# One conditional block ahead of the expert slots in place of four behind them

## Chip, cores, metric

One Trainium2 chip, one core. The metric is device time in microseconds of one execution.

## What is computed

Three stages in a row, all in float32 at the interface (the second MLP's weights come as float64):

```python
# 1: attention, q, k, v: [4, 8, 576, 64]
out_d = softmax_attention(mean of 4 tokens of q, of k, of v)      # 144 tokens
scores = np.where(abs(i - j) < 4, scale * q @ k.T, -1e9)
attn_out = repeat(out_d, 4) + softmax(scores) @ v
x = attn_out.transpose(0, 2, 1, 3).reshape(2304, 512)
# 2: mixture of 8 experts, one expert per row
e_idx = argmax(x @ w_gate + modality_bias[modality_id])
for e in range(8):
    h = np.maximum(x[e_idx == e] @ w1[e], 0)                        # 512 -> 1024
    out[e_idx == e] = gate_w * (h @ w2[e])                          # 1024 -> 512
# 3: MLP 512 -> 2048 -> 512
h = out @ w_in
g = np.maximum(h, 0) + alpha * np.minimum(h, 0)
return g @ w_out
```

## The kernel before

Line numbers are those of the kernel before.

**Attention** (to L371) yields after each tile of 96 tokens; it writes each row with its gate to a table in DRAM (xs), sorted by expert. Beside it class `Early` (L569 to L596) already works out slots of 128 rows of the leading expert (ph and py are its matmuls, L583).

**Plan.** At the end of the attention `Router.plan` (L444 to L498) counts the rows of each expert on DVE, and writes a table of integers (r_tab): for each slot of 256 rows its expert, its first row, where its result goes, and, in row 4, how many slots there are. Engines read single values of it into registers (`reg`, `finish`).

**Slots** (`moe`, L598 to L673). A slot is 256 rows of one expert. There are always seven (NSU = 7); up to 16 can occur (NSM), if the rows fall badly over the experts. [...] A slot: load its rows (L, L554), times the gates on POOL (L560), transpose on DVE (T, L562), split (xh, xl); eight groups h of 12 matmuls of 128x256 (L648), relu into hh and hl; four groups y of 24 (L667). 8 x 12 + 4 x 24 = 192 matmuls. Its eight pieces of w1 and eight of w2 are split one by one, a little ahead of their use; the raw weights of the next expert (wraw) are loaded into the same buffer as soon as a part is split. For slot 0 the leading expert's raw weights lie there since the attention.

**Input weights.** `W2in(i)` (L802 to L807) brings one of 32 pieces (128x256) of w_in through a ring of three buffers, makes a float32 of the float64 in three DVE operations (xwi, `from64`, L537 to L539), and splits it into wih (ACT) and wil (POOL). Each slot asks for six pieces (L654), behind its first six h groups; the scheduler puts them where operands and buffers allow.

**The end of the slots.** Behind slot 6 (L817 to L820) stand three conditional blocks for the slots past the seventh, and a fourth that loads the second MLP's first block of rows again if few early slots were done. With the data of the case none is taken. All five engines carry each block's instructions, so each branches over them.

**Second MLP** (`moe2`, L694 to L747): five blocks of rows; per block 16 groups oh (12 matmuls of 128x512, L723) and the products oy (L714). Output weights are converted during block 0.

The instruction order on each engine is set by a list scheduler at build time, within priorities (`high_priority`); conditional blocks are barriers that it doesn't move work across.

```python
            for s in range(NSU):
                if s==2: load()
                slot(s)
            for u in range(2): w_out_rows(0,u)
            # slots that are rarely there, in groups; one without rows does no harm
            for a,b in [[NSU,NSU+1],[NSU+1,NSU+3],[NSU+3,NSM]]:
                with tc.If(nb>a):
                    for s in range(a,b): slot(s)
            with tc.If(done<BLOCKS[0][1]//SE): load()
```

Of the kernel before, what the change touches and what calls it, by code (L numbers as in the profile page):

```python
# [14 lines left out]

def attention(ctx, tc, q, k, v, mod, wg, bias, xs, running, ps, eps, zeros, filler):
    """Attention, gating and the scatter of the rows by expert; yields after each token tile."""
# [87 lines left out]
    # routing constants  # L105
# [73 lines left out]
    def softd(b,name,e,p,n):  # L179
        """exp and the factors; p: n heads of scores"""  # L180
# [8 lines left out]
    def stageB(b,pair):  # L189
        """queries 0-127 of two heads"""  # L190
# [8 lines left out]
    def stageT(b):  # L199
        """the queries past 128 of all heads, on partitions (h,i)"""  # L200
# [75 lines left out]
    def local2(b,t):  # L276
        """values, the sum of both attentions"""
# [11 lines left out]
    def gate2(b,t):  # L289
        """rows and their experts"""  # L290
# [23 lines left out]
    def gate3(b,t):  # L314
        """to their places"""
# [20 lines left out]
    def down(b):  # L336
        """the work that a sequence needs before its tiles, in small steps"""
# [3 lines left out]
    # prologue  # L341
# [32 lines left out]
LEAD=1; WLOAD=tuple([0, 0, 1, 2, 2, 3, 3, 4]); EARLY=tuple([3, 6, 10, 14, 16]); ETAIL=0  # L374
F=1024; F2=2048; SL=256; SE=128; NSP=len(EARLY); NK=N//SL; NSU=-(-(N-SE*NSP)//SL); NSM=N//SL+E-1   # early slots of SE rows; slots always there, at most
ENG=mybir.EngineType

class Router:
    """Slots of 256 rows of one expert, worked out on partition 0."""
    def __init__(self, tc, rp, cp):  # L380
# [24 lines left out]
        self.done=rp.tile([1,1],I32,name="r_done"); self.tab0=rp.tile([1,4],I32,name="r_tab0")  # L405
# [4 lines left out]
    def lead(self, psum, running):  # L410
        """the expert with the most rows so far goes first"""
# [10 lines left out]
    def early(self, psum, running, k):  # L422
        """whether the leading expert has SE*(k+1) rows by now, and where they begin"""
# [7 lines left out]
        # SE*k rows into its own rows, or the zeros behind them all  # L431
# [4 lines left out]
    def early_rows(self):  # L436
        """rows of the leading expert that were worked out early"""
        nc=self.nc; dn=self.dn=self.cp.tile([1,1],F32,name="r_dn")
        nc.vector.tensor_reduce(out=dn,in_=self.ok[:,1:],axis=AX.X,op=ALU.add)
        nc.vector.tensor_copy(self.done,dn)  # L440
        nc.vector.tensor_scalar(out=dn,in0=dn,scalar1=float(SE),scalar2=None,op0=ALU.mult)
    def plan(self, psum, running, cp):
# [3 lines left out]
        nr=w([1,2,E],"nr")            # slots and rows of each expert, in the order of the slots  # L446
# [39 lines left out]
        xr=w([1,NSM],"xr")            # its rows; the zeros where there is no slot  # L486
# [10 lines left out]
        nc.vector.tensor_copy(tab[:,4,0:1],sb[:,2,E-1:E])  # L497
        nc.vector.tensor_copy(tab[:,5:7],y[:,5:7])     # where zeros go behind fewer rows than a slot's  # L498
    def reg(self, row, s, engines, hi):
        t=self.tab[0:1,row*NSM+s:row*NSM+s+1]  # L500
        if s==0 and row in (1,2,5,6): i=(1,2,5,6).index(row); t=self.tab0[0:1,i:i+1]
        return self.nc.values_load(t,engines=engines,min_val=0,max_val=hi,
            skip_runtime_bounds_check_because="follows from the row counts")
    def finish(self, engines):
        return self.nc.values_load(self.done[0:1,0:1],engines=engines,min_val=0,max_val=NSP,
            skip_runtime_bounds_check_because="a count of early slots")

class Weights:
    """One expert's weights as they come, and the parts of each chunk of 128 hidden units."""
# [4 lines left out]
    def load1(self, part, e, cond=None):  # L514
        """part 0-3: a quarter of the hidden units"""
# [4 lines left out]
    def load2(self, part, e, cond=None):  # L520
        """part 0-3: a quarter of the columns"""
# [5 lines left out]
def split(nc, hi, lo, x, lo_engine):  # L527
    """x as the sum of two parts of 12 bits each"""
# [3 lines left out]
def from64(nc, pool, name, hi, lo, raw, lo_engine):  # L532
    """float64 bits to the two parts of the float32 they give"""
# [8 lines left out]
class Rows:  # L542
    """Rows of one expert, and their result's way out."""
# [13 lines left out]
    def turn(self, pool, L, name, n):  # L557
        """times the gates, transposed"""
# [10 lines left out]
class Early:  # L569
    """Slots of the leading expert while the attention still runs, in float32 as it is."""  # L570
# [27 lines left out]
def moe(tc, stack, router, wts, rows, ep, W2in):  # L598
# [6 lines left out]
    def load_x(s):  # L605
        rows.zeros(router.reg(5,s,[ENG.SP],E*N),router.reg(6,s,[ENG.SP],1))
        xin[s]=rows.load(wk,router.reg(1,s,[ENG.SP],E*N),str(s),SL,2)
        rows.tokens(xin[s],router.reg(2,s,[ENG.SP],N),SL)
    def prep_x(s):
        L=xin[s]; T=rows.turn(wk,L,str(s),SL)  # L610
        hi=wk.tile([128,4,SL],F32R,tag="xh",name=f"xh{s}"); lo=wk.tile([128,4,SL],F32R,tag="xl",name=f"xl{s}")
# [10 lines left out]
    W1={}; W2={}  # L622
    def slot(s):
        last=s+1==NSM
        if s==0:
            with tc.high_priority(0): load_x(0); prep_x(0)
            load_x(1)
        if s>=NSU and not last: load_x(s+1)
# [4 lines left out]
        def one(s,f):  # L633
            if f<8 and (s,f) not in W1 and s<NSM: W1[s,f]=split1(s,f)
# [5 lines left out]
        for f in range(8):  # L640
# [32 lines left out]
    return slot  # L673
# [20 lines left out]
def moe2(tc, stack, wp, fp, ep, win, first, W2out, al, ysT, ytok, out):  # L694
# [12 lines left out]
    def block(j):  # L707
# [9 lines left out]
        for f in range(16):  # L717
# [13 lines left out]
            # the last block finishes its rows one half after the other  # L731
# [118 lines left out]
```

## Time and profile before

| | |
|---|---|
| median of 3 runs | 894.38 us (890.66 to 899.22) |
| span of the profiled execution | 888.4 us |
| mean granted TensorE clock | 0.959 |
| PE busy | 815.4 us (92%) |
| DVE busy | 535.3 us (60%) |
| ACT busy | 362.1 us (41%) |
| POOL busy | 267.5 us (30%) |
| data moved by DMA | 72.39 MB |

Of the profiled execution the span is given, from its first to its last instruction; the three timed runs lie 2.3 to 10.8 us above it. Engines: PE matmul, PEld its weight load, DVE vector, ACT scalar, POOL general, SP issues DMAs. A "q" behind an engine's name is its sequencer, which takes branches and semaphores. "[3.87 <-DVE T L562]" behind an instruction: its engine was idle 3.87 us ahead of it, until DVE's operation on T at L562 ended. "issue" stands for idle time in which the engine waited for nothing that the profile shows.

### The profile page before, as it was taken

How to read it: one execution, taken by the hardware profiler on the slowest of the kernel's cores; microseconds unless marked ns; L12 is line 12 of the kernel's file. 1: busy time of each engine (PE TensorE's matmuls, PEld its weight loads, DVE VectorE, ACT ScalarE, POOL GpSimd, SP SyncE). 2: the span in 40 equal slices, each digit the busy share in tenths (PEclk: the TensorE clock that was granted, in tenths of full speed). 3: DMA queues.
4: the chain of work that ended last, by engine and by line, in shares of the span. 5: the costliest groups of instructions: out<-in, count | busy, mean ns of one | idle time of the engine just before them, and what ended most of it. 6: DMA issues, size and time to landing. Idle time of an engine off the chain costs nothing. (4 is left out here: it accounts for less than half of the span.)

```text
span 888.4 us, 16892 instructions
## 1 busy us (share of the span) xinstructions
PE 815.4 (92%) x6175; PEld 697.4 (78%) x6175; DVE 535.3 (60%) x1297; ACT 362.1 (41%) x864; POOL 267.5 (30%) x451
## 2 busy tenths in 40 slices
PE   5797899998997898999994999999999999999997
PEld 3565688777997898999993888888888888888895
DVE  6856756665356799997744998353345333533361
ACT  8688795984342464664631332211121111111120
POOL 9325546464463355444402332100010001000100
PEclk9878889999999999999996999999999999999999
DMA  7635674322234543349202351200020001000000
GB/s 190 169 94 165 184 221 124 93 60 65 56 86 109 109 120 92 100 127 282 47 29 75 114 158 61 83 13 1 0 78 13 1 1 53 13 1 0 36 14 24
DMA packets 97978, 72.39 MB, mean 81 GB/s; under 512 B 40792, under 2 KB 85336, under 8 KB 97880
## 3 DMA queue, kind: packets, MB, share of 16 engines
q1 hardware_dynamic: 94904, 61.56, 25.6%
q0 software_dynamic: 2976, 9.59, 3.2%
q8 instruction: 54, 0.88, 0.5%
q14 instruction: 44, 0.36, 0.2%
HBM read 81.17 MB, written 19.44 MB: 113 GB/s over the span
## 5 line engine op out<-in xcount | busy, mean ns | idle before, releaser
L529 ACT CAST gh<-m 128x512 fp32r<-128x512 f32 (+1 forms) x80 | 44.5, 557 | 246.1 <-DVE m L726 241.2
L723 PE MATMUL oh<-oxh,wih 128*128 128x512 f32 (+1 forms) x320 | 120.1, 375 | 14.1 <-issue 14.1
L723 PE MATMUL oh<-oxh,wil 128*128 128x512 f32 (+1 forms) x320 | 119.8, 374 | 0.0
L723 PE MATMUL oh<-oxl,wih 128*128 128x512 f32 (+1 forms) x320 | 119.5, 373 | 0.0
L725 DVE TENSOR_SCALAR m<-oh,al 128x512 f32<-128x512 f32 (+1 forms) x80 | 55.5, 694 | 94.2 <-PE oh L723 94.2
L740 POOL DMA_INDIRECT out<-o,ti x18 | 17.6, 979 | 312.8 <-ACT o L739 276.4
L714 PE MATMUL oy<-woh,gh 128*128 128x512 f32 x272 | 107.2, 394 | 0.0
L714 PE MATMUL oy<-wol,gh 128*128 128x512 f32 x272 | 106.7, 392 | 0.0
L714 PE MATMUL oy<-woh,gl 128*128 128x512 f32 x272 | 106.4, 393 | 0.0
L723 PEld LDWEIGHTS oh<-oxh,wih 128*128 128x128 f32 x320 | 60.8, 190 | 25.9 <-issue 14.3
L648 PE MATMUL h<-xh,w1h 128*128 128x256 f32 x224 | 64.5, 289 | 13.1 <-DVE hl L651 11.4
L530 DVE TENSOR_TENSOR gl<-m,gh 128x512 fp32r<-128x512 f32 (+1 forms) x80 | 49.3, 616 | 40.8 <-ACT gh L529 40.8
L723 PEld LDWEIGHTS oh<-oxh,wil 128*128 128x128 f32 x320 | 60.7, 190 | 12.1
L723 PEld LDWEIGHTS oh<-oxl,wih 128*128 128x128 f32 x320 | 60.8, 190 | 11.5
L648 PE MATMUL h<-xl,w1h 128*128 128x256 f32 x224 | 63.9, 286 | 0.0
L648 PE MATMUL h<-xh,w1l 128*128 128x256 f32 x224 | 63.8, 285 | 0.0
L667 PE MATMUL y<-hh,w2h 128*128 128x256 f32 x224 | 61.5, 285 | 0.0
L667 PE MATMUL y<-hh,w2l 128*128 128x256 f32 x224 | 61.0, 284 | 0.2 <-DVE w2l L530 0.2
L714 PEld LDWEIGHTS oy<-woh,gl 128*128 128x128 f32 x272 | 51.1, 188 | 12.0
L714 PEld LDWEIGHTS oy<-wol,gh 128*128 128x128 f32 x272 | 51.0, 188 | 11.4
L714 PEld LDWEIGHTS oy<-woh,gh 128*128 128x128 f32 x272 | 51.1, 188 | 11.0
L667 PE MATMUL y<-hl,w2h 128*128 128x256 f32 x224 | 58.7, 284 | 0.7 <-DVE hl L651 0.7
(296 smaller groups left out, 1880.9 us busy)
## 6 DMA issues: line engine op xcount, KB each, us to landing
wraw<-in_moe_w SPq DMA_DIRECT2D x64, 512.0 KB
wi<-in_moe_w_in SPq DMA_DIRECT2D x32, 256.0 KB
wo<-in_moe_w_out SPq DMA_DIRECT2D x32, 256.0 KB
vw<-in_v SPq DMA_DIRECT2D x88, 64.0 KB
xs<-z SPq DMA_DIRECT2D x9, 528.0 KB
L<-xs SPq DMA_DIRECT2D x32, 132.0 KB
ldq<-in_q SPq DMA_DIRECT2D x16, 256.0 KB
ldk<-in_k SPq DMA_DIRECT2D x16, 256.0 KB
```

Source lines behind the costliest of these rows:

```text
L529: nc.scalar.copy(hi,x)
L530: lo_engine.tensor_tensor(out=lo,in0=x,in1=hi.bitcast(F32),op=ALU.subtract)
L648: nc.tensor.matmul(h,lhsT=a[:,c],rhs=b[:,c],start=n==0,stop=n==11); n+=1
L667: nc.tensor.matmul(y,lhsT=a[:,f],rhs=b,start=n==0,stop=n==23); n+=1
L714: nc.tensor.matmul(y[t],lhsT=a[:,ts],rhs=b[:,f],start=f==0 and k==0,stop=f==15 and k==2)
L723: nc.tensor.matmul(h[:,:n],lhsT=a[:,c,fs],rhs=b[:,c,:n],start=k==0,stop=k==11); k+=1
L725: nc.vector.tensor_scalar(out=m[:,:n],in0=h[:,:n],scalar1=0.0,scalar2=al[:,f:f+1],op0=ALU.min,op1=ALU.mult)
L740: nc.gpsimd.indirect_dma_start(out=out[:],out_offset=bass.IndirectOffsetOnAxis(ap=ti[:,t:t+1],axis=0),in_=o[:],in_offset=None,bounds_check ...
```

## The change

Lines of the changed kernel are named as such.

- The four blocks behind slot 6 go. In their place one flag, `rare`, is worked out in the plan: 1 if there are more than seven slots or fewer than four early slots. One block, `with tc.If(rare>0): every()`, stands **ahead of slot 0**. `every()` works out all 16 slots from scratch (`whole`), each with its own loads and splits, and then loads slot 0's weights again. If the flag is set, the table sends the results of the seven slots that follow to a place behind all rows.
- The rows of slot 0 (`first0`: load, gates, transpose, split) and eight pieces of input weights (AT0 = 8) stand ahead of the block; a slot's six pieces count on from the eighth, and pieces run from the last quarter of w_in's rows to the first.
- The order of instructions is made anew by the scheduler. The eight early splits of slot 0's w1 and w2, which stood among the plan's operations, stand behind the block now, since the block writes the raw weights.
- Slot 6 asks for no rows and weights of an eighth slot; slot 0's place for results is read from the plan's last table.

```diff
@@ plan
+        rf=w([1,4],"rf")
+        nc.vector.tensor_reduce(out=rf[:,0:1],in_=nr[:,0],axis=AX.X,op=ALU.add)
+        nc.vector.tensor_scalar(out=rf[:,0:1],in0=rf[:,0:1],scalar1=float(NSU),scalar2=None,op0=ALU.is_gt)
+        nc.vector.tensor_scalar(out=rf[:,1:2],in0=dn,scalar1=float(BLOCKS[0][1]),scalar2=None,op0=ALU.is_lt)
+        nc.vector.tensor_tensor(out=rf[:,2:3],in0=rf[:,0:1],in1=rf[:,1:2],op=ALU.max)
+        nc.vector.tensor_copy(self.rare,rf[:,2:3])
...
-        nc.vector.tensor_tensor(out=tab[:,2],in0=yr,in1=st,op=ALU.add)
+        nc.vector.tensor_tensor(out=yr,in0=yr,in1=st,op=ALU.add)
+        nc.vector.tensor_copy(tab[:,7],yr)
+
+        nc.vector.tensor_scalar(out=xr,in0=yr,scalar1=-1.0,scalar2=float(N),op0=ALU.mult,op1=ALU.add)
+        nc.vector.scalar_tensor_tensor(out=tab[:,2],in0=xr,scalar=rf[:,2:3],in1=yr,op0=ALU.mult,op1=ALU.add)
@@ moe
+    def first():
+        with tc.high_priority(0): load_x(0); L=xin[0]; prep_x(0)
+        rows.tokens(L,router.reg(2,0,[ENG.SP],N),SL)
+    def every():
+
+        x0=xin.pop(0)
+        for s in range(NSM): whole(s,router.reg(0,s,[ENG.SP],E-1))
+        xin[0]=x0
+        e=router.reg(0,0,[ENG.SP],E-1)
+        for i in range(4): wts.load1(i,e); wts.load2(i,e)
     def slot(s):
-        last=s+1==NSM
-        if s==0:
-            with tc.high_priority(0): load_x(0); prep_x(0)
-            load_x(1)
-        if s>=NSU and not last: load_x(s+1)
+        last=s+1==NSU
+        if s==0: load_x(1)
...
-            if s<NSU and f<6: W2in(6*s+f)
+            if f<6: W2in(AT0+6*s+f)
             if f==4 and not last: prep_x(s+1)
-            if f==5 and s+2<=NSU and s+2<NSM: load_x(s+2)
+            if f==5 and s+2<NSU: load_x(s+2)
@@ body
             def W2in(i):
-                c,p=divmod(i,8); ps=slice(256*p,256*p+256)
-                if c>3: return
+                c,p=divmod(i,8); c=3-c; ps=slice(256*p,256*p+256)
+                if c<0: return
...
-            nb=router.reg(4,0,(ENG.Pool,ENG.Activation,ENG.PE,ENG.DVE,ENG.SP),NSM)
-            slot=moe(tc,s1,router,wts,rows,ep,W2in)
+            rare=router.flag((ENG.Pool,ENG.Activation,ENG.PE,ENG.DVE,ENG.SP))
+            slot,first0,every=moe(tc,s1,router,wts,rows,ep,fp,W2in)
             load,first=rows2(tc,fp,ep,ysT,ytok,0)
-            done=router.finish((ENG.Pool,ENG.Activation,ENG.PE,ENG.DVE,ENG.SP))
+            first0()
+            for i in range(AT0): W2in(i)
+            with tc.If(rare>0): every()
             for s in range(NSU):
                 if s==2: load()
                 slot(s)
             for u in range(2): w_out_rows(0,u)
-
-            for a,b in [[NSU,NSU+1],[NSU+1,NSU+3],[NSU+3,NSM]]:
-                with tc.If(nb>a):
-                    for s in range(a,b): slot(s)
-            with tc.If(done<BLOCKS[0][1]//SE): load()
```

What stands on DVE ahead of the block in the changed kernel (xl is slot 0's low part; xwi are pieces of input weights, numbered by their buffer's use; L549 is the third operation of a piece):

```order
L540 TENSOR_TENSOR xl_4455<-T_4452,xh_4454 128x1024
L547 TENSOR_SCALAR xwi_4520<-wi_4518 128x256
L548 SCALAR_TENSOR_TENSOR xwi_4520<-wi_4518,xwi_4520 128x256
L547 TENSOR_SCALAR xwi_10130<-wi_10128 128x256
L549 SCALAR_TENSOR_TENSOR xwi_4520<-wi_4518,xwi_4520 128x256
L548 SCALAR_TENSOR_TENSOR xwi_10130<-wi_10128,xwi_10130 128x256
L549 SCALAR_TENSOR_TENSOR xwi_10130<-wi_10128,xwi_10130 128x256
L547 TENSOR_SCALAR xwi_10160<-wi_10158 128x256
L548 SCALAR_TENSOR_TENSOR xwi_10160<-wi_10158,xwi_10160 128x256
L547 TENSOR_SCALAR xwi_10193<-wi_10191 128x256
L549 SCALAR_TENSOR_TENSOR xwi_10160<-wi_10158,xwi_10160 128x256
L548 SCALAR_TENSOR_TENSOR xwi_10193<-wi_10191,xwi_10193 128x256
```

Directly behind these DVE reads the flag and takes the branch (L515 and L860 of the changed kernel): ten whole pieces and two thirds of an eleventh stand ahead of it. On DVE of the kernel before, around the same xl, there are seven pieces up to the first low part of w1 that stands behind it:

```order
L562 STREAM_TRANSPOSE T_4455<-L_4445 128x1024
L537 TENSOR_SCALAR xwi_4690<-wi_4688 128x256
L538 SCALAR_TENSOR_TENSOR xwi_4690<-wi_4688,xwi_4690 128x256
L539 SCALAR_TENSOR_TENSOR xwi_4690<-wi_4688,xwi_4690 128x256
L530 TENSOR_TENSOR xl_4458<-T_4455,xh_4457 128x1024
L537 TENSOR_SCALAR xwi_4914<-wi_4912 128x256
L538 SCALAR_TENSOR_TENSOR xwi_4914<-wi_4912,xwi_4914 128x256
L539 SCALAR_TENSOR_TENSOR xwi_4914<-wi_4912,xwi_4914 128x256
L562 STREAM_TRANSPOSE T_4655<-L_4471 128x1024
L530 TENSOR_TENSOR w1l_3_4524<-wraw,w1h_3_4523 128x512
```

The first three low parts of w1 (w1l_0 to w1l_2) are missing in these rows because they stand among the plan's operations further up; in the changed kernel w1l_0 is the second operation behind the block.

On PE of the kernel before, the end of the slots (y_3 is the last group of slot 6, oh_0 the first of the second MLP; of each long block the branch's second half is shown):

```order
L667 MATMUL y_3_10257<-hl_7_10163,w2h_31_10214 128x256
L818 UNCONDITIONAL_BRANCH x2
L505 TENSOR_LOAD r_done
L820 COMPARE_AND_BRANCH
L820 UNCONDITIONAL_BRANCH x2
L723 MATMUL oh_0_10342<-oxh_4425,wih 128x512
```

And of the changed kernel, the same place:

```order
L714 MATMUL y_2_12632<-hl_7_12564,w2h_21_12581 128x256
L770 MATMUL oh_0_12727<-oxh_4433,wih 128x512
L770 MATMUL oh_0_12727<-oxl_4434,wih 128x512
L770 MATMUL oh_0_12727<-oxh_4433,wil 128x512
L770 MATMUL oh_0_12727<-oxh_4433,wih 128x512
L714 MATMUL y_3_12658<-hh_0_12404,w2h_30_12597 128x256
```

No branch stands there any more, and four matmuls of oh_0 come ahead of y_3.

## Rows read from the trace of the kernel before

**Rows 1.** Page: busy time, share of the span and instructions of each engine.

```profile
PE 815.4 (92%) x6175; PEld 697.4 (78%) x6175; DVE 535.3 (60%) x1297; ACT 362.1 (41%) x864; POOL 267.5 (30%) x451
```

**Rows 2.** Waits: line <- what it waited for, us in total, times, longest.

```profile
POOL wol L530 <- PEq L818: 32.4, 1, 32.4
...
PE oh L723 <- issue: 14.1, 1, 14.1
```

**Rows 3.** Timeline of PE around 470 us: start, us, instruction.

```profile
464.45 0.28 PE L667 MATMUL y<-hl,w2h 128*128 128x256 f32 x1
478.82 0.77 PE L723 MATMUL oh<-oxh,wih 128*128 128x512 f32 x1 [14.08 <-issue]
```

**Rows 4.** Chain that ended last, in order of time: one of its groups of 12.

```profile
498.09 2.80 PE oh L723 x12
```

**Rows 5.** Instructions of line L818: ns min/median/max, first and last start in us.

```profile
L818 ACTq EVENT_SEMAPHORE  x3: 17/17/17, 462.6 to 466.2; - x3
L818 PEldq COMPARE_BRANCH  x3: 3917/4943/4987, 463.0 to 472.4; - x3
L818 DVEq COMPARE_BRANCH  x3: 56/56/72, 465.4 to 466.4; - x3
L818 DVEq EVENT_SEMAPHORE  x3: 21/21/21, 465.6 to 470.2; - x3
```

**Rows 6.** Instructions of line L820, PE's sequencer.

```profile
L820 PEldq COMPARE_BRANCH  x1: 233/233/233, 477.9 to 477.9; - x1
```

**Rows 7.** Windows, slots 0 to 5 and after the hole: length, busy by engine, PEclk, DMA.

```profile
284.65:313.91 29.26, 25.41 (x209) 25.01 (x209) 22.86 (x42) 15.00 (x34) 9.46 (x8) 1.00 0.45 99
313.91:340.04 26.13, 23.80 (x194) 23.20 (x193) 25.99 (x43) 14.70 (x35) 15.59 (x13) 1.00 0.40 113
340.04:367.81 27.77, 24.87 (x195) 24.66 (x193) 26.43 (x46) 15.12 (x35) 15.20 (x14) 0.94 0.40 115
367.81:393.53 25.72, 24.19 (x194) 23.31 (x193) 25.35 (x50) 15.75 (x36) 10.41 (x11) 1.00 0.40 128
393.53:418.49 24.96, 23.30 (x194) 23.09 (x193) 20.40 (x33) 15.43 (x34) 12.03 (x10) 1.00 0.92 241
418.49:441.53 23.04, 23.04 (x194) 23.04 (x193) 17.06 (x26) 13.85 (x28) 9.86 (x7) 1.00 0.33 71
...
478.82:484.07 5.25, 5.25 (x12) 4.11 (x13) 4.21 (x11) 1.22 (x3) 1.71 (x3) 0.50 0.32 101
```

**Rows 8.** The same windows, tile xwi alone: DVE, ACT, POOL, PEclk, DMA (slots 0, 1, 3).

```profile
284.65:313.91 29.26, 7.17 (x18) 2.04 (x5) 4.59 (x5) 1.00 0.45 99
313.91:340.04 26.13, 13.00 (x19) 2.85 (x7) 6.32 (x7) 1.00 0.40 113
...
367.81:393.53 25.72, 10.37 (x22) 2.85 (x7) 7.62 (x8) 1.00 0.40 128
```

**Rows 9.** Timelines of ACT, SP, POOL, DVE and PE ahead of slot 0.

```profile
256.81 1.66 ACT L529 CAST w1h<-wraw 128x512 fp32r<-128x512 f32 x3
...
273.16 1.91 SPq L554 DMA_DIRECT2D L<-xs  x4
...
280.62 1.95 SPq L806 DMA_DIRECT2D wi<-in_moe_w_in  x2
...
280.33 1.91 POOL L560 TENSOR_TENSOR L<-L 128x1024 f32<-128x1024 f32 x1 [3.24 <-DMA L<-xs]
...
276.54 0.83 DVE L539 SCALAR_TENSOR_TENSOR xwi<-wi,xwi 128x256 int32<-128x256 int32 x1
282.28 1.25 DVE L562 STREAM_TRANSPOSE T<-L 128x1024 f32<-128x1024 f32 x1 [4.91 <-POOL L L560]
284.00 0.29 DVE L537 TENSOR_SCALAR xwi<-wi 128x256 int32<-128x256 int32 x1 [0.48 <-DMA wi<-in_moe_w_in]
...
277.43 5.52 PE L583 MATMUL py<-eh,wraw 128*128 128x128 f32 x48
284.65 0.63 PE L648 MATMUL h<-xh,w1h 128*128 128x256 f32 x3 [1.70 <-ACT xh L529]
```

More of the change, by code (lines that the diff above doesn't have):

```diff
@@ L373, in attention @@
     loading.close()
[L374 removed]
+LEAD=1; WLOAD=tuple([0, 0, 1, 2, 2, 3, 3, 4]); EARLY=tuple([3, 6, 10, 14, 16]); AT0=8
 F=1024; F2=2048; SL=256; SE=128; NSP=len(EARLY); NK=N//SL; NSU=-(-(N-SE*NSP)//SL); NSM=N//SL+E-1
@@ L404, in __init__ @@
         self.xr=rp.tile([1,NSP],I32,name="r_xr"); self.ok=c([1,NSP+1],"r_ok"); nc.vector.memset(self.ok[:,0:1],1.0)
-        self.done=rp.tile([1,1],I32,name="r_done"); self.tab0=rp.tile([1,4],I32,name="r_tab0")
+        self.rare=rp.tile([1,1],I32,name="r_rare"); self.tab0=rp.tile([1,4],I32,name="r_tab0")
     def counts(self, psum, running):
@@ L439, in early_rows @@
         nc.vector.tensor_reduce(out=dn,in_=self.ok[:,1:],axis=AX.X,op=ALU.add)
-        nc.vector.tensor_copy(self.done,dn)
         nc.vector.tensor_scalar(out=dn,in0=dn,scalar1=float(SE),scalar2=None,op0=ALU.mult)
@@ L451, in plan @@
         nc.vector.tensor_scalar(out=X[:,2],in0=nr[:,1],scalar1=-float(SL),scalar2=0.0,op0=ALU.add,op1=ALU.max)
-        f=w([1,4],"f0")
+        f=w([1,4],"f0"); nc.vector.memset(f,0.0)
         nc.vector.tensor_tensor(out=f[:,1:2],in0=X[:,2,0:1],in1=dn,op=ALU.min)
@@ L500, in reg, with flag @@
         t=self.tab[0:1,row*NSM+s:row*NSM+s+1]
-        if s==0 and row in (1,2,5,6): i=(1,2,5,6).index(row); t=self.tab0[0:1,i:i+1]
+        if s==0 and row in (1,5,6): i=(1,2,5,6).index(row); t=self.tab0[0:1,i:i+1]
         return self.nc.values_load(t,engines=engines,min_val=0,max_val=hi,
             skip_runtime_bounds_check_because="follows from the row counts")
-    def finish(self, engines):
-        return self.nc.values_load(self.done[0:1,0:1],engines=engines,min_val=0,max_val=NSP,
-            skip_runtime_bounds_check_because="a count of early slots")
+    def flag(self, engines):
+        return self.nc.values_load(self.rare[0:1,0:1],engines=engines,min_val=0,max_val=1,
+            skip_runtime_bounds_check_because="a flag")
 class Weights:
@@ L596, in finish, with moe @@
     def finish(self): self.go(len(self.steps))
-def moe(tc, stack, router, wts, rows, ep, W2in):
+def moe(tc, stack, router, wts, rows, ep, fp, W2in):
     nc=tc.nc
@@ L604, in moe, with load_x, tokens, prep_x @@
     xin={}
-    def load_x(s):
+    def load_x(s, out=2, name=""):
         rows.zeros(router.reg(5,s,[ENG.SP],E*N),router.reg(6,s,[ENG.SP],1))
[L607 to L611, printed above, removed]
+        xin[s]=rows.load(wk,router.reg(1,s,[ENG.SP],E*N),f"{name}{s}",SL,2)
+        if s or name: tokens(s,out)
+    def tokens(s, out=2): rows.tokens(xin[s],router.reg(out,s,[ENG.SP],N),SL)
+    def prep_x(s, name=""):
+        L=xin[s]; T=rows.turn(wk,L,f"{name}{s}",SL)
+        if name:
+            hi=fp.tile([128,4,512],F32R,tag="xh",name=f"xh{name}{s}")[:,:,:SL]; lo=fp.tile([128,4,512],F32R,tag="xl",name=f"xl{name}{s}")[:,:,:SL]
+        else:
+            hi=wk.tile([128,4,SL],F32R,tag="xh",name=f"xh{name}{s}"); lo=wk.tile([128,4,SL],F32R,tag="xl",name=f"xl{name}{s}")
         split(nc,hi,lo,T,nc.vector)
@@ L622, in moe, with whole @@
     W1={}; W2={}
-    def slot(s):
-        last=s+1==NSM
-        if s==0:
-            with tc.high_priority(0): load_x(0); prep_x(0)
-            load_x(1)
-        if s>=NSU and not last: load_x(s+1)
+    def whole(s, e):
+        for i in range(4): wts.load1(i,e); wts.load2(i,e)
+        load_x(s,7,"r"); prep_x(s,"r"); xh,xl=xin.pop(s)
+        H=[]
+        for f in range(8):
+            wh,wl=split1(f"r{s}",f)
+            h=hp.tile([128,SL],F32,tag="h",name=f"hr{s}_{f}")
+            for c in range(4):
+                for k,(a,b) in enumerate(((wh,xh),(wh,xl),(wl,xh))):
+                    nc.tensor.matmul(h,lhsT=a[:,c],rhs=b[:,c],start=c==0 and k==0,stop=c==3 and k==2)
+            hh=wk.tile([128,SL],F32R,tag=f"hh{f}",name=f"hhr{s}_{f}",bufs=1); hl=wk.tile([128,SL],F32R,tag=f"hl{f}",name=f"hlr{s}_{f}",bufs=1)
+            nc.scalar.activation(out=hh,in_=h,func=AF.Relu)
+            nc.vector.scalar_tensor_tensor(out=hl,in0=h,scalar=0.0,in1=hh.bitcast(F32),op0=ALU.max,op1=ALU.subtract)
+            H.append((hh,hl))
+        o=ep.tile([128,4,SL],F32,tag="eh",name=f"yor{s}",bufs=1)
+        for c in range(4):
+            y=yp.tile([128,SL],F32,tag="y",name=f"yr{s}_{c}")
+            for u in range(2):
+                wh,wl=split2(f"r{s}",c,u)
+                for f in range(4):
+                    hh,hl=H[4*u+f]
+                    for k,(a,b) in enumerate(((wh,hh),(wl,hh),(wh,hl))):
+                        nc.tensor.matmul(y,lhsT=a[:,f],rhs=b,start=u==0 and f==0 and k==0,stop=u==1 and f==3 and k==2)
+            nc.vector.tensor_copy(o[:,c],y)
+        rows.store(o,router.reg(7,s,[ENG.SP],N),SL)
+    def first():
[6 more added lines that the diff above has]
+        e=router.reg(0,0,[ENG.SP],E-1)
+        for i in range(4): wts.load1(i,e); wts.load2(i,e)
+    def slot(s):
+        last=s+1==NSU
+        if s==0: load_x(1)
         if not last:
@@ L633, in one @@
         def one(s,f):
-            if f<8 and (s,f) not in W1 and s<NSM: W1[s,f]=split1(s,f)
+            if f<8 and (s,f) not in W1: W1[s,f]=split1(s,f)
         def two(i):
@@ L672, in slot @@
         rows.store(o,yr,SL)
-    return slot
+    return slot,first,every
 BLOCKS=[(512*j,512) for j in range(4)]+[(2048,256)]
```

1 line of the change is left out of this document (removed).

## Prediction, made before the changed kernel had run

> **What bounds the kernel now.** I read the page's totals first, then the waits, then the chain that ended last, then the timeline at the places these named. TensorE (PE) is busy 92% of the span [rows 1], so only two things can make the kernel shorter: PE's holes, and stretches in which PE runs under its pace. The largest hole stands in the list of waits: before the first matmul of the second MLP (oh, L723) PE stood 14.1 us once, and what ended it is named "issue", that is, no other engine's work; POOL waited 32.4 us for PE's sequencer at L818 as well [rows 2]. The timeline puts the hole between the last y matmul at 464.45 and the first oh at 478.82 [rows 3]. From there to the end the chain is PE alone, in groups of 12 matmuls of 2.80 us [rows 4], so what goes here comes off the end one for one. What fills the hole is read from the instructions of L818: PE's sequencer took three compare-and-branches of 3917 to 4987 ns each, between 463.0 and 477.4 [rows 5]: 3.9 + 4.9 + 5.0 = 13.8 of the 14.1. Their neighbour at L820, which skips only a short block, took 233 ns [rows 6]. So the price is not the comparison but the landing behind a long skipped block, and there are three long ones.
>
> The other stretch is the seven slots (284.65 to 464.73). Each has 192 matmuls. Slot 5 takes 23.04 with PE busy all of it, so that is the floor; slots 0 to 4 take 29.26, 26.13, 27.77, 25.72 and 24.96, with DVE busy 25 to 26 of it in slots 1 to 3 [rows 7]. There DVE is the bound, and what loads it is the conversion of the input weights (xwi): 13.00 us of slot 1's 25.99 [rows 7, 8].
>
> **What the change removes.** All four blocks leave the end of slot 6, so PE goes from y to oh without a branch, and the hole of 14.09 goes. [...] Would something else be late there? The first oh reads the ready rows (oxh) and the ready input weights, which slots 2 to 3 left behind; the first output weights are wanted only after four more groups, 11 us on. I count the whole 14.09 + 2.45 = 16.54. If a quarter of it came back as a wait for output weights, 4 us.
>
> [...]
>
> **What it adds.** One block stands ahead of slot 0, on all five engines, and skips more instructions than any of the three. Its price, from branch to what follows it: PE 3.9 to 5.0 a branch; DVE 3.8, from its last compare at 466.4 to its last semaphore at 470.2 [rows 5]. A block as long as the new one stands in no row; its price is bounded by L820's 0.2 and PE's 5.0, and I take DVE's 3.8, since DVE will be the last.
>
> [...]
>
> Who is last at the block? PE's early matmuls run to 283 (48 from 277.43 on [rows 9]), a last group of 16 takes some 2 more, and its branch (5.0) is over by 290. SP has to issue twelve weight pieces, and DVE has to convert ten and two thirds of them ahead of the block, with the rows' transpose (T) and their low part (xl). DVE is the last. Now five pieces are done before T (the last operation at 276.54), and T ends at 282.28 + 1.25 = 283.5 [rows 9]; 17 operations are left. At 0.40 each (7.17 for 18 in slot 0, [rows 8]) that is 6.8, and xl is another pass like T, 1.25: DVE reaches the branch at 291.5 if nothing fits in ahead of T. From the transfers: a piece takes 3.4 from its issue (280.62) to its first operation (284.00) [rows 9], three buffers go round; the eighth is done near 286, the eleventh is issued then, lands at 289.4, and its two operations end at 290.2. I take 290.5. Bounds: with the pieces fully ahead of T, 286.5; with operations at slot 1's 0.68 (13.00 for 19) and a transfer like that of the rows, 5.3 from the last issue (275.07) to POOL's start (280.33) [rows 9], 297.
>
> Behind it: 290.5 + 3.8 + one cast of a slot's weights (1.66 for three, 0.55) = 294.9 for slot 0's first matmul, where it is now 284.65 [rows 9]. The eight weight splits of slot 0 that now run beside the plan (the first three casts at 256.81 [rows 9]) come behind the block too, since the block would overwrite the weights. So slot 0 is like slot 1, which makes all its splits and seven pieces in 26.13 (slot 0 after the change has six and a third), plus a cold start. PE will have been idle for 12 us; after the 14 us hole the clock was 0.50 for 5.25 us. In a slot with 3 us of slack (26.13 against 23.04) half of the lost 2.45 shows: 27.5. Slot 0 then ends at 322.4, and not at 313.91: +8.5. Bounds of its length: 24.5 (a slot hardly bound by DVE) and 30.7 (now's length and the cold part).
>
> **What it moves.** Seventeen pieces are done by the end of slot 0, where now ten are; slots 1 and 2 take seven each as before, slot 3 one in place of seven or eight, slot 4 none. Slot 3's 10.37 us of xwi on DVE [rows 8] go, all but 1.2, and it falls from 25.72 to about PE's floor: 23.4, -2.3. Slot 4 holds only 24.96 - 23.04 = 1.9 over the floor and was rid of pieces anyway: -0.2. Slots 1 and 2 I leave as they are (bounds: -3 to +2).
>
> Sum: -16.54 + 8.5 - 2.5 = -10.5 on the profiled span of 888.4, so 877.9 there. The three timed runs lie 2.3 to 10.8 above that span, their median 6.0; the same difference from the median 894.38 gives 883.9.
>
> **The rivals.**
> 1. *Late block* (no change that can be told). DVE or a late piece brings the block to 297, slot 0 starts at 301.4 and takes 27.5: it ends 15 later than now. -16.54 + 15 - 2.5 = -4: 890. For it: DVE operations reached 0.68 on average in slot 1 where other engines share its data. Against: ahead of slot 0 there is little else running.
> [...]
> 3. *More than counted.* Pieces ahead of T, the block reached at 286.5, slot 0 at 291 with 25: it ends at 316, +2. -16.54 + 2 - 2.5 = -17: 877. For it: DVE had 4.91 of idle before T.
> 4. *The hole stays.* What stood 14.1 us is not the branches, or output weights take their place: then +8.5 - 2.5 = +6, 900. Against: 13.8 of the 14.1 are branch records. That the block is taken, because the new flag is set, I set aside: sixteen slots at 23 us or more would be over 360 us, and now the same conditions were not met.
>
> **How the numbers follow.** Forecast 0.50 (883.9, its own range 878 to 889), late block 0.21, serial fetches 0.07, more than counted 0.17, the hole stays 0.05. One per cent, 8.9 us, is about what a measurement of this kernel can tell from no change. Faster by more (under 885.4): two thirds of the forecast, rival 3, a little of rival 1: 0.52. Slower by more (over 903.3): 0.07. The rest 0.41. The range goes from 873 (rival 3 and 4 us of the runs' scatter) to 896 (rival 1 with slots 1 and 2 two worse and the scatter).
>
> **What would show it right or wrong.** In the profile after: no wait of the first oh for "issue", y followed by oh within 0.3 us, and oh at full clock from its first group. One compare-and-branch on PE of 4 to 6 us near 283; DVE's branch near 290; slot 0's first h at 295; a low clock in its first 5 us; slot 0 of 27 to 28; slot 3 near 23.4. The forecast is wrong if h starts before 291 or after 299, if slots 1 and 2 change by over 2, or if a wait of some other kind stands before oh or oy.

## The result and the profile after

The changed kernel takes 884.25 us (median of 4 runs, 883.44 to 884.79); the kernel before, beside it, 894.08 (890.66 to 899.22). The ratio is 0.9882, 95% interval 0.9848 to 0.9915. The prediction was 883.9. The profiled span fell by less, from 888.4 to 882.2, that is by 6.2 and not by 9.8 us: where these 3.6 us lie is one of the questions below.

To set beside [rows 2], two rows of the waits after; the first oh no longer appears among them:

```profile
POOL wol L540 <- PE y L714: 21.6, 1, 21.6
...
DVE xwi L547 <- DMA wi<-in_moe_w_in: 13.8, 5, 7.5
```

To set beside [rows 3], the timeline of PE where the hole was (start, us, instruction): four oh stand ahead of the last y group, the rest directly behind it, all at a granted clock of 1.00 (0.40 each in place of 0.77).

```profile
472.16 0.28 PE L714 MATMUL y<-hl,w2h 128*128 128x256 f32 x1
472.28 0.40 PE L770 MATMUL oh<-oxh,wih 128*128 128x512 f32 x1
...
475.96 0.28 PE L714 MATMUL y<-hl,w2h 128*128 128x256 f32 x1
476.08 0.40 PE L770 MATMUL oh<-oxl,wih 128*128 128x512 f32 x1
```

To set beside [rows 5], the instructions of the new block's line (ns min/median/max, first and last start). Each engine branches once; between the compare and the first semaphore behind it, the landing, lie 2.9 us on DVE and 2.7 on ACT.

```profile
L860 PEldq COMPARE_BRANCH  x1: 3527/3527/3527, 286.2 to 286.2; - x1
...
L860 DVEq COMPARE_BRANCH  x1: 72/72/72, 292.8 to 292.8; - x1
L860 ACTq COMPARE_BRANCH  x1: 50/50/50, 293.0 to 293.0; - x1
L860 DVEq EVENT_SEMAPHORE  x1: 21/21/21, 295.7 to 295.7; - x1
L860 ACTq EVENT_SEMAPHORE  x1: 17/17/17, 295.7 to 295.7; - x1
```

To set beside [rows 9], timelines ahead of slot 0 (first and last operation of the plan, SP's issues, POOL's rows, the sixth piece, the first operation behind the block, slot 0's first matmul):

```profile
256.29 0.17 DVE L447 TENSOR_TENSOR r_t<-r_A,cnt 1x64 f32<-1x64 f32 x1
...
269.93 0.22 DVE L504 SCALAR_TENSOR_TENSOR r_tab<-r_xr,r_rf,r_yr 1x16 int32<-1x16 f32 x1
...
272.82 0.35 SPq L575 DMA_DIRECT2D ytok<-L  x1
273.27 16.01 SPq L853 DMA_DIRECT2D wi<-in_moe_w_in  x6
...
275.75 1.91 POOL L570 TENSOR_TENSOR L<-L 128x1024 f32<-128x1024 f32 x1 [2.33 <-DMA L<-xs]
...
282.03 0.29 DVE L547 TENSOR_SCALAR xwi<-wi 128x256 int32<-128x256 int32 x1 [7.54 <-DMA wi<-in_moe_w_in]
...
295.81 0.43 DVE L549 SCALAR_TENSOR_TENSOR xwi<-wi,xwi 128x256 int32<-128x256 int32 x1 [3.01 <-DVEq L860]
...
296.62 0.58 PE L695 MATMUL h<-xh,w1h 128*128 128x256 f32 x1 [7.31 <-ACT w1h L539]
```

To set beside [rows 7], the windows of slots 0 to 4 and of what follows slot 6 (length, busy by engine, clock, DMA):

```profile
296.62:324.64 28.02, 25.80 (x192) 25.38 (x193) 28.02 (x42) 15.35 (x33) 15.35 (x11) 0.91 0.45 95
324.64:351.98 27.34, 24.97 (x195) 24.65 (x194) 26.64 (x45) 16.56 (x40) 15.85 (x13) 0.94 0.39 94
351.98:378.82 26.84, 24.77 (x195) 24.57 (x194) 24.61 (x48) 15.42 (x35) 14.21 (x14) 0.94 0.48 128
378.82:404.62 25.80, 24.06 (x194) 23.24 (x193) 22.57 (x41) 16.61 (x36) 10.59 (x10) 1.00 0.44 131
404.62:429.08 24.46, 23.30 (x195) 23.10 (x194) 15.41 (x26) 13.06 (x28) 8.96 (x6) 1.00 0.76 199
...
475.97:487.50 11.53, 11.53 (x53) 9.50 (x52) 10.69 (x23) 2.79 (x6) 3.80 (x5) 1.00 0.34 115
```

To set beside [rows 8], the tile xwi alone in slots 0 and 3 (DVE, ACT, POOL, clock, DMA):

```profile
296.62:324.64 28.02, 7.51 (x16) 2.02 (x5) 4.56 (x5) 0.91 0.45 95
...
378.82:404.62 25.80, 4.74 (x7) 1.22 (x3) 2.88 (x3) 1.00 0.44 131
```

Slot 0 has DVE busy all of its 28.02. Slot 3 lost about half of its conversion (xwi on DVE 4.74 in place of 10.37) and is as long as before, 25.80 against 25.72.

One table serves all that follows. It cuts each profile at four places read from timelines: the plan's first operation on DVE, its last write to r_tab, slot 0's first matmul, slot 6's last y. The first column is attention, the same code in all but e9. The rest begins at the last y; except in before, e1 and e6, four oh (0.9 us) stand ahead of that y and count in the slots.

| | plan starts | plan | plan to slot 0 | seven slots (slot 0) | rest | span |
|---|---|---|---|---|---|---|
| before | 257.1 | 16.0 | 11.5 | 179.8 (29.2) | 423.9 | 888.4 |
| after | 256.3 | 13.9 | 26.5 | 179.3 (28.0) | 406.2 | 882.2 |
| e1 before again | 258.5 | 16.3 | 9.6 | 185.1 (33.7) | 423.8 | 893.3 |
| e6 one behind | 257.3 | 16.3 | 9.5 | 184.8 (33.6) | 413.7 | 881.7 |
| e7 none behind | 253.1 | 16.2 | 10.3 | 186.6 (32.9) | 406.2 | 872.5 |
| e2 no block | 255.3 | 17.0 | 14.9 | 180.0 (28.0) | 406.2 | 873.3 |
| e3 short block | 252.1 | 13.5 | 20.3 | 181.6 (26.9) | 406.2 | 873.8 |
| e11 one slot in it | 259.9 | 13.8 | 24.3 | 178.2 (28.6) | 406.2 | 882.4 |
| e4 tokens last | 261.8 | 13.8 | 24.6 | 183.3 (28.1) | 406.0 | 889.5 |
| e5 AT0 = 0 | 257.5 | 14.6 | 24.7 | 182.9 (27.8) | 406.3 | 886.0 |
| e8 five, pinned | 258.5 | 13.6 | 19.7 | 189.2 (30.5) | 406.2 | 887.2 |
| e12 eight, pinned | 255.2 | 14.0 | 25.6 | 185.0 (27.0) | 406.2 | 886.0 |
| e9 ahead of early | 264.8 | 12.7 | 20.0 | 188.1 (35.1) | 406.2 | 891.8 |
| e10 at the end | 255.4 | 16.9 | 15.1 | 180.6 (27.4) | 409.8 | 877.8 |

Each row is one profile. As attention alone spreads from 252 to 262, spans are best compared without it, from the plan's start to the end: before 631.3, e1 634.8, after 625.9, e6 624.4, e7 619.4, e2 618.0, e3 621.7, e11 622.5, e9 627.0, e10 622.4.

### The profile page after: what moved, and what is told of

It reads as the page before. It is cut to its first block, busy times and chain, and to the rows that moved or that the text cites. A ratio compares the mean times of both kernels' runs of the same rounds, so it can differ in the third digit from the quotient of the medians.

```text
span 882.2 us, 16794 instructions
## 1 busy us (share of the span) xinstructions
PE 814.7 (92%) x6175; PEld 698.2 (79%) x6175; DVE 530.3 (60%) x1302; ACT 360.6 (41%) x863; POOL 261.8 (30%) x450
## 4 chain that ended last, share of the span: by engine, by line
PE 57%; DVE 3%; DMA 2%; issue 2%; SPq 0%; POOL 0%; POOLq 0%; ACT 0%; DVEq 0%; ACTq 0%
PE oh L770 23%; PE oy L761 22%; PE h L695 7%; PE y L714 5%; DVE w2l L540 1%; DMA L<-xs 1%; DMA wi<-in_moe_w_in 1%; DVE w1l L540 1%; DVE xwi L548 1%; DVE hl L698 0%; DMA ytok<-L 0%; DMA oT<-ysT 0%; DMA out<-o,ti 0%; DVE xwi L549 0%; DVE oxl L540 0%
## 5 line engine op out<-in xcount | busy, mean ns | idle before, releaser
L787 POOL DMA_INDIRECT out<-o,ti x18 | 17.6, 976 | 308.9 <-ACT o L786 271.3
L695 PE MATMUL h<-xh,w1h 128*128 128x256 f32 x224 | 66.4, 297 | 15.2 <-DVE hl L698 7.9
L770 PEld LDWEIGHTS oh<-oxh,wih 128*128 128x128 f32 x320 | 60.1, 188 | 11.5
L714 PE MATMUL y<-hl,w2h 128*128 128x256 f32 x224 | 59.6, 285 | 0.9 <-DVE hl L698 0.9
```

The costliest lines, as they stand in the source:

```text
L695: nc.tensor.matmul(h,lhsT=a[:,c],rhs=b[:,c],start=n==0,stop=n==11); n+=1
L714: nc.tensor.matmul(y,lhsT=a[:,f],rhs=b,start=n==0,stop=n==23); n+=1
L770: nc.tensor.matmul(h[:,:n],lhsT=a[:,c,fs],rhs=b[:,c,:n],start=k==0,stop=k==11); k+=1
L787: nc.gpsimd.indirect_dma_start(out=out[:],out_offset=bass.IndirectOffsetOnAxis(ap=ti[:,t:t+1],axis=0),in_=o[:],in_offset=None,bounds_check ...
```

## Experiments

Times are medians; in brackets the ratio to the kernel before on the same chip, with its 95% interval. The intervals reach 3 to 4 us to either side, so a difference of some microseconds between two versions is told by the times only roughly; the profiles say where it lies. My theory A: a long skip is paid by what waits behind it, and the change moves one such price ahead of slot 0. Rivals stand with the runs.

**e1, the kernel before again.** No edit.

> The kernel before, unchanged, for the spread of its own runs. Its first three runs lie at 890.7, 894.4 and 899.2 us with a profiled span of 888.4; the profile after is only 6.2 us shorter (882.2), the medians 9.8. Theory A: the hole between y and oh is as long in every run (14 us), and the spread comes from elsewhere in the program; ratio to before 1.00, spans 888 to 895. [...]

894.8 us (1.001, 0.998 to 1.004), spans 888 to 899 in twelve runs. The hole was 13.60, as before:

```profile
483.38 0.76 PE L723 MATMUL oh<-oxh,wih 128*128 128x512 f32 x1 [13.60 <-issue]
...
284.38:318.08 33.70, 28.40 (x211) 27.89 (x210) 22.94 (x43) 15.59 (x35) 10.29 (x9) 0.90 0.42 90
```

The second row is the window of slot 0: 33.70, and not 29.26 as in [rows 7]; e6 and e7, with the same slots, have 33.6 and 32.9. In e1 PE was busy 28.40 of it at a mean clock of 0.90, in the first profile 25.41 at 1.00. So the spread is not in the hole: attention ends some microseconds sooner or later, and the profiled slot 0 of before was a short one. From the plan's start to the end e1 takes 3.5 longer than the first profile: that is where the 3.6 us lie.

**e6, one block behind; e7, none.**

```diff
-            for a,b in [[NSU,NSU+1],[NSU+1,NSU+3],[NSU+3,NSM]]:
+            for a,b in [[NSU,NSM]]:                    # e6; e7: without these lines
                 with tc.If(nb>a):
                     for s in range(a,b): slot(s)
-            with tc.If(done<BLOCKS[0][1]//SE): load()
+                    load()
```

> The kernel before with its four blocks behind slot 6 made one (nine slots and the load in one block, at the same place; the load is left out where only it would be wanted). Theory A (the price is one landing per long skip): one compare-and-branch of 4 to 5 us on PE in place of 13.8, hole of 5 to 6 us, and a shorter low clock: 9 us less than before, ratio 0.990. Rival B (the number of skipped instructions sets the price): hole stays near 14, ratio 1.00. If it is as fast as the change (0.988), then the change's gain is the merging and its place brings nothing.

> The kernel before without its four blocks; the slots past the seventh and the second load are left out, which this data doesn't take. Theory A: the hole of 14.1 us and the low clock behind it go and nothing takes their place: 16.5 us less, ratio 0.9815, oh within 0.3 us of y. Rival: a wait for output weights (POOL, ACT) appears that the hole hid; then 10 to 13 less.

e6: 884.8 us (0.989, 0.986 to 0.993). Hole and branch (timeline of PE, and line L818):

```profile
472.14 0.77 PE L723 MATMUL oh<-oxh,wih 128*128 128x512 f32 x1 [3.89 <-DVEq L818]
...
L818 PEldq COMPARE_BRANCH  x1: 3672/3672/3672, 466.5 to 466.5; - x1
...
L818 DVEq COMPARE_BRANCH  x1: 72/72/72, 468.9 to 468.9; - x1
...
L818 PEldq EVENT_SEMAPHORE  x1: 51/51/51, 470.3 to 470.3; - x1
L818 DVEq EVENT_SEMAPHORE  x1: 21/21/21, 471.9 to 471.9; - x1
```

e7: 878.1 us (0.984, 0.980 to 0.989), no hole; its rest is 17.6 shorter than e1's. Both came as theory A had it, but that e6's hole is shorter than its 5 to 6. On PE the price here went by the number of long skips, not by the instructions skipped: three skips of one, two and six slots took 3.9 to 5.0 us each [rows 5], one skip of all nine took 3.7. PE has landed at 470.3; what its first oh still waits for is DVE, which branched later and landed at 471.9. e6's rest is 7.5 longer than e7's: 0.9 of it is the four oh that e7 has in slot 6, the other 6.6 are the hole (4.2 from the last y at 467.97 to 472.14) and the slow start behind it (the first two oh took 0.77 and 0.63, in e7 0.40 and 0.39). And e6 is as fast as the change. **Merging four blocks into one brings the gain; moving the one ahead of the slots brings nothing on top that these times can tell.** One block behind costs 6.7 by medians (e6 less e7).

**e2, the change without its block.**

```diff
-            with tc.If(rare>0): every()
```

> The changed kernel without its block ahead of slot 0 (the rare case is left out). Theory A: the block costs some 8 to 11 us ahead of slot 0; without it the splits of slot 0 go back beside the plan, slot 0 starts 8 to 10 us earlier (287 to 289), and the time is 874 to 876, about that of the kernel before without blocks. Rival C: the late start is the pieces of input weights put ahead, not the block: then slot 0 starts at 293 or later and the time is 880 or more.

876.7 us (0.982, 0.978 to 0.987), and slot 0 started at 287.15, as theory A had it. So ahead of slot 0 the block costs 884.25 - 876.7 = 7.5 by medians, and 7.9 in the profiles from the plan's start to the end. In the table: plan 3.1 shorter with the block (the splits of slot 0's weights, each a cast of a high part on ACT and a subtraction for a low part, are gone from it), way to slot 0 11.6 longer.

**e3 and e11, the block made short.** e3 keeps only the loads in the block, e11 one slot of 16:

```diff
-        for s in range(NSM): whole(s,router.reg(0,s,[ENG.SP],E-1))      # e3
-        for s in range(NSM): whole(                                     # e11
+        for s in range(1): whole(
```

> The changed kernel with a short block at the same place: the 16 recomputed slots are left out, only the eight loads of raw weights stay in it (data of this case doesn't take it). The scheduler puts 8 pieces ahead of it in place of 10 2/3. Theory A (the price is the landing behind a long skip, 3.0 on DVE and ACT): DVE branches near 290 and goes on 0.3 later, slot 0 starts at 290 to 291 (after: 296.6), time 878 to 880. Rival (the price is the barrier, the splits kept behind it): slot 0 starts at 294 or later, 882 to 884.

> The changed kernel with one of the 16 recomputed slots in the block (the other 15 are left out; data of this case doesn't take the block). DVE's order ahead of the block is the same as after, ten pieces and two thirds. DVE's skip falls from some 420 instructions to 26, PE's from 3073 to 193. Theory A (the landing is a matter of the skip's length on each engine): DVE and ACT go on within 0.5 us, PE's landing of 3.5 to 5 is over by 291, slot 0 starts at 293.5 to 294.5, time 880 to 882. Rival (the late start is all DVE's pieces and the barrier): slot 0 at 296, 883 to 885.

e3: 876.9 us (0.987, 0.983 to 0.992; four of its six runs lie at 875 to 877, two at 883 to 884), slot 0 at 285.9, faster than theory A had it. e11: 884.8 us (0.988, 0.985 to 0.992). In e11 DVE and ACT went on at once, while PE, with some 193 matmuls to skip, reached its semaphore only 3.1 after its branch (3.6 after; line L860):

```profile
L860 PEldq COMPARE_BRANCH  x1: 353/353/353, 289.8 to 289.8; - x1
L860 PEldq EVENT_SEMAPHORE  x1: 51/51/51, 292.9 to 292.9; - x1
...
L860 DVEq COMPARE_BRANCH  x1: 72/72/72, 296.4 to 296.4; - x1
L860 DVEq EVENT_SEMAPHORE  x1: 21/21/21, 296.6 to 296.6; - x1
L860 ACTq COMPARE_BRANCH  x1: 50/50/50, 296.6 to 296.6; - x1
L860 ACTq EVENT_SEMAPHORE  x1: 17/17/17, 297.1 to 297.1; - x1
```

Plan to slot 0 is 24.3 in place of 26.5: the landing on DVE and ACT is worth 2.2 there. The time doesn't show it: 884.8 lies in the rival's range and not in theory A's, in a profile whose plan began 3.6 later; from the plan's start to the end e11 is 3.4 shorter than the change. In e3, with 8 2/3 pieces ahead and no landing to speak of (DVE branched at 284.7 and went on at 284.9, PE's branch record has 228 ns), plan to slot 0 is 20.3, against 14.9 without a block (e2); from the plan's start to the end e3 takes 3.7 more than e2 and 4.2 less than the change. So the profiles give about half of the block's cost to what the barrier keeps behind it and to DVE's pieces, and half to the landings. By medians e3 is as fast as e2 and e11 as slow as the change, so these shares are argued and not shown.

**e4, tokens behind the pieces.**

```diff
-        rows.tokens(L,router.reg(2,0,[ENG.SP],N),SL)
+        return lambda: rows.tokens(L,router.reg(2,0,[ENG.SP],N),SL)
...
-            first0()
+            tok0=first0()
             for i in range(AT0): W2in(i)
+            tok0()
```

> The changed kernel with the token numbers of slot 0 (1 KB in pieces of 4 bytes, issued at 272.8 between the rows and the sixth piece) stored behind the pieces. In the profile after DVE stood 7.5 us until the sixth piece had come (282.03), though it was issued at 273.3. Theory A (the tokens hold up what is queued behind them): that wait falls to 2 to 3 us, DVE branches 3 to 5 earlier, slot 0 starts at 292 to 294, time 880 to 882. Rival (the tokens only move the same hold to the next pieces, or the gain ahead comes back in slots that DVE bounds): 884 +- 2.

885.7 us (0.991, 0.988 to 0.994). The wait of 7.54 for the sixth piece became 0.43, but later pieces wait (2.14 on the eighth), and DVE branched 20.8 after the plan's end in place of 22.7, and slot 0 started 24.6 after it in place of 26.5. The rival was right: no gain in the time.

**e5, no pieces asked for ahead.**

```diff
-AT0=8
+AT0=0
```

> The changed kernel with no piece of input weights asked for ahead of the block (AT0 = 0); the scheduler takes ten of slots 0 and 1 ahead of it all the same. Theory A: nothing ahead of slot 0 changes (DVE branches at 291 to 293, slot 0 at 295 to 297), the time stays at 884 +- 2. Rival (that eight are asked for ahead is what relieves the slots): slots 0 to 3 longer by 4 to 6, 888 to 890.

884.0 us (0.991, 0.987 to 0.994): no change. The eight pieces "prepared ahead" are not what fills the stretch: the scheduler takes ten of the later slots' pieces across the block anyway. (The description ahead of the prediction says that it moves nothing across; that holds only for what conflicts with the block, as the splits do.)

**e8 and e12, fewer pieces ahead.** The loads of slot 0's six pieces are kept in program order, with AT0 = 5 (e8) and 8 (e12):

```diff
-                nc.sync.dma_start(r.rearrange("p d w -> p (d w)"),...)
+                d=nc.sync.dma_start(r.rearrange("p d w -> p (d w)"),...)
+                if AT0<=i<AT0+6: tc.keep_in_program_order(d)
```

> The changed kernel with five pieces ahead (AT0 = 5) and the loads of the next six kept in program order, so that six and not eleven stand ahead of the block on DVE. Theory A (DVE's queue of pieces makes the block late): DVE branches at 281 to 284, PE is last, slot 0 starts at 286 to 289, 8 to 10 earlier; some 6 us of conversion go back into slots that DVE bounds, about half of it on the path: 878 to 881. Rival (the pieces are hidden there, what is saved ahead comes back in full): 884 +- 2.

> The changed kernel with the loads of slot 0's six pieces kept in program order, so that nine pieces and not ten and two thirds stand ahead of the long block, nearly as many as with the short block (eight and two thirds: slot 0 at 285.9, 877 us). Theory A (short and long block differ by the landing): DVE branches at 285 to 287, slot 0 starts at 289 to 291, time 880 to 882. Rival (what is saved ahead comes back in slots 0 and 1, as with six pieces): 884 to 887.

e8: 887.0 us (0.993, 0.989 to 0.997), a miss of theory A; the rival had the cause right and the time 1 us too low. Slot 0 starts 6.7 sooner after the plan, and slots 0 and 1 take it back (windows; 28.02 and 27.34 after):

```profile
291.80:322.28 30.48, 26.60 (x192) 25.96 (x193) 25.61 (x41) 14.25 (x31) 13.69 (x9) 0.90 0.50 88
322.28:353.86 31.58, 26.35 (x194) 25.74 (x193) 26.92 (x47) 18.35 (x42) 16.32 (x14) 0.89 0.44 90
```

e12: 891.1 us (0.998, 0.995 to 1.001), a miss of both theories: the way to slot 0 hardly shrank (25.6), and slots 1 and 3 took 32.1 and 30.3, with single waits of PE for DVE's hl of up to 4.1. Pinning changes the order of all that follows, so e12 tells nothing clean about the landing.

**e9, the block ahead of the last early slot.** The fifth early slot's matmuls are held back until behind the block, which follows the plan directly (shown is the order; the edit also holds the early steps back and moves one buffer of the rare case):

```diff
-            first0()
-            for i in range(AT0): W2in(i)
-            with tc.If(rare>0): every()
+            with tc.If(rare>0): every()
+            early.finish()
+            first0()
+            for i in range(AT0): W2in(i)
```

> The changed kernel with the block directly behind the plan, ahead of the last early slot's matmuls, of slot 0's rows and of the pieces; slot 0's raw weights are the leading expert's, which the block loads again at its end, so nothing else changes. Theory A (the block costs what it holds up): PE lands behind its branch while it would wait for the plan, 32 + 32 early matmuls and slot 0's splits follow beside the rows' transfer, slot 0 starts at 285 to 289 as without a block, time 875 to 879. Rival (any block costs 7 us of all engines wherever it stands): 882 to 885.

896.3 us (1.006, 1.002 to 1.009), slower than before and outside both theories. PE lost what had filled its time beside the plan (8.11 idle, then 5.62 behind the branch), and DVE's pieces came to lie in slot 0 (35.1):

```profile
276.60 3.65 PE L593 MATMUL ph<-Te,wraw 128*128 128x128 f32 x16 [8.11 <-DVE r_tab L496]
285.86 7.70 PE L593 MATMUL ph<-Te,wraw 128*128 128x128 f32 x48 [5.62 <-ACT eh L598]
```

From the plan's start to the end, though, e9 takes only 1.1 more than the change (627.0 against 625.9). Most of what it lost lies ahead of the plan, which began at 264.8, later than in any other profile; no run here shows why.

**e10, the block at the very end.** The rare case is worked out after the second MLP, and then the second MLP again (`every` also loses its last loads of slot 0's weights):

```diff
-            with tc.If(rare>0): every()
...
             moe2(tc,s2,wp,fp,ep,(wir,wil),first,W2out,al,ysT,ytok,out)
+        rare=router.flag((ENG.Pool,ENG.Activation,ENG.PE,ENG.DVE,ENG.SP))
+        with tc.If(rare>0):
+            with ExitStack() as s3:
+                moe(tc,s3,router,Weights(tc,wp,w1,w2),rows,ep,fp,W2in)[2]()
+            with ExitStack() as s4:
+                load,first=rows2(tc,fp,ep,ysT,ytok,0); load()
+                moe2(tc,s4,wp,fp,ep,(wir,wil),first,W2out,al,ysT,ytok,out)
```

> The changed kernel without its block ahead of slot 0; in its place one block behind the second MLP, which in the rare case works out all slots and the second MLP again. All of the computation is kept. Theory A (the landing costs what waits behind it, and there is little at the end): slots as without a block, and 0 to 4 us at the end: 876 to 881. Rival (the engines' landing of 3 to 5 us adds up at the end, behind the last store): 882 to 886.

879.9 us (0.985, 0.981 to 0.988), the shortest of the versions that keep the whole computation, 4.3 below the change by medians (the intervals of the two ratios overlap) and 3.5 in the profiles from the plan's start to the end. Its slots are about as long as those of e2 (180.6 and 180.0); at the end 3.6 are left (rest 409.8 against 406.2). PE's branch record of 3.6 us, from 864.2 on, lies beside matmuls that run to 867.9; POOL's first semaphore, at 872.0, comes behind its last store, issued from 868.9 to 869.9 (line L863).

```profile
L863 POOLq EVENT_SEMAPHORE  x5: 17/43/43, 872.0 to 872.3; - x5
...
L863 PEldq COMPARE_BRANCH  x1: 3561/3561/3561, 864.2 to 864.2; - x1
...
L863 POOLq COMPARE_BRANCH  x1: 53/53/53, 869.2 to 869.2; - x1
```

## Why the prediction was right, and where it was not

**The hole and its cold start** (16.54 forecast): right. The 2.45 in it is what the first 12 oh took, 5.25 at a granted clock of 0.50 [rows 7], less the 2.80 of a later group [rows 4]; after, the clock is 1.00 from the first oh on. The rest shrank by 423.9 - 406.2 = 17.7, of which 0.9 is the four oh now in slot 6: 16.8. No wait took its place; e7 shows the same without any block.

**The later start of slot 0** (10.25 forecast): too small. In the two profiles it is 12.0, and 13 to 14 for plan and way together (40.3 after; 27.5 in before and 25.9 in e1). The landing was over-counted (3.8; DVE 3.0); PE was over by 290, as forecast (289.8). The way to the block was under-counted: DVE branched at 292.8 and not at 290.5, though its plan had ended 3.0 sooner than before. The sixth piece came 8.8 after its issue and not 3.4, and T, whose rows were ready at 277.7, stood behind it in DVE's order: T ended 13.8 after the plan, where before it was 10.4. Behind T the forecast had 8.05 for 17 operations and xl; 15 were left and took 8.9, with two waits of 0.62 for POOL's wil. Moving the tokens (e4) moves the wait for the piece and doesn't end it.

**The slots** (slot 0 down 1.8, slot 3 down 2.3, slot 4 down 0.2): against e1 the seven slots became 5.8 shorter where the forecast had 4.3, but in another place. The step that failed is "slot 3 ... falls from 25.72 to about PE's floor", -2.3; it fell by nothing. First, only 15 pieces were done by the end of slot 0 and not 17, so that slot 3 kept 4.74 us of xwi on DVE and not 1.2. Second, its windows cut in halves, before and after, show where the relief went:

```profile
367.81:380.00 12.19, 10.66 (x82) 9.78 (x81) 12.19 (x21) 7.34 (x16) 5.45 (x6) 1.00 0.28 89
380.00:393.53 13.53, 13.53 (x115) 13.53 (x114) 13.16 (x31) 8.41 (x21) 4.96 (x5) 1.00 0.52 162
```

```profile
378.82:391.00 12.18, 10.44 (x81) 9.62 (x80) 12.15 (x20) 6.97 (x16) 7.08 (x6) 1.00 0.34 100
391.00:404.62 13.62, 13.62 (x115) 13.62 (x115) 10.43 (x22) 9.64 (x21) 3.51 (x4) 1.00 0.53 158
```

DVE is busy all of the first half; the second runs at PE's pace in both. The pieces went out of the second half (13.16 to 10.43), where DVE had been off the path. A busy share over a whole slot hid that. What became shorter was slot 0: 33.7, 33.6 and 32.9 in three profiles of the old slots, 28.0 after and 28.6 in e11 with the same order. The forecast took the 29.26 of one profile for the rule. But part of this is only a shifted mark: in the old order slot 0's first three matmuls stand ahead of the last 16 of the early slot, which then count in slot 0 (209 to 211 matmuls in place of 192), as in the kernel before:

```profile
285.12 1.95 PE L583 MATMUL py<-eh,wraw 128*128 128x128 f32 x16
```

In e2, without any block, slot 0 starts 4.6 later after the plan than in e7 and is 4.9 shorter. (One bound of slot 0's length was added up wrongly: now's length and the cold part are 29.26 + 2.45 = 31.7, not 30.7. Nothing else hangs on it.)

**The total** came out right partly because errors cancel. A mark that both orders share is the end of slot 0. Counted from the plan's start it lies at 68.4 after, and at 59.4 to 59.6 in e1, e6 and e7 (56.8 in the first profile): 8.7 to 9.0 later, where the forecast had 8.5, made up of a start that was later and a slot 0 that was shorter than forecast. Slots 1 to 6, without the four oh, became 0.2 to 1.0 shorter against the first profile, e1 and e6 (2.4 against e7), where the forecast had 2.5. Against e1 the terms measured are -16.6 + 8.7 - 1.0 = -8.9, where the forecast had -16.54 + 8.5 - 2.5 = -10.5 and the medians gave -9.8. That the median came within 0.4 us of the forecast is luck at that size: runs of the kernel before spread by 9 us. Of the rivals, "late block" had the place right (2.3 late at the branch) and not its weight; what the chances call "serial fetches" (0.07; the engines' landings one after another, and a slower kernel) fell: the five engines branched between 286.2 and 293.0, and DVE and ACT landed together at 295.7. "The hole stays" fell with the profile after and with e7.

**What the change is worth by its parts:** three long skips and a short one made into one long skip, about 10 (e6: 884.8); the one left costs 6.7 behind and 7.5 ahead by medians, so no gain can be told from its new place.

## What to carry to other kernels

Count the long conditional skips on a path and merge them (here three and a short one into one: about 10 us, e6); then put the one that is left where the least work waits behind it, which here, by the medians and the profile of e10, is the program's end. Before crediting relief to a stage, cut it in halves and see in which half the relieved engine bounds it. Where run times spread by 1%, take a second profile of the kernel before, and compare stage by stage from a common mark.

## What the runs showed of the hardware that was not expected

The landing hit engines differently by the length of their own skip: with one slot in the block (e11) DVE and ACT went on after 0.2 and 0.5 us, with sixteen after 2.9 and 2.7; why, no run shows. On PE a skip of everything (3527 to 6038 ns over the runs with a long block ahead of slot 0) was not clearly dearer than one of nine slots behind (3672), and with one slot the branch record fell to 353 ns while the semaphore still came 3.1 us after the branch.

The profile counts the transfers of instructions by themselves (queue; packets, MB, share of the transfer engines' time). The kernel before, with three long skips, has 98 packets, and without any block (e7) 83:

```profile
q8 instruction: 54, 0.88, 0.5%
q14 instruction: 44, 0.36, 0.2%
```

```profile
q8 instruction: 49, 0.80, 0.4%
q14 instruction: 34, 0.28, 0.1%
```

With one long block there are 92 (e6) or 91 (after, e10); with none ahead of slot 0 there are 81 (e2), and with a short one 83 (e3) and 84 (e11). So long skips went with more packets of instructions in these runs; that the engines waited for just these is not shown, as the view gives no times.

A transfer of 1 KB in pieces of 4 bytes, issued ahead of 256 KB loads by the same engine, went with a wait of 7.5 to 7.8 us for the next load in six profiles, and moving it only moved the wait; whether the small pieces or the many loads set it was not settled.
